# Chunk 0's decays summed in PSUM instead of passed through DRAM, the beginning reordered, and the check of the weights moved to later chunks

## The chip, the core and the metric

The kernel runs on one core of a Trainium2 chip. The metric is the device time of one execution in microseconds (us), median over runs. Names: PE is TensorE, DVE is VectorE, ACT is ScalarE, POOL is GpSimd, SP is SyncE, which here only issues DMAs. Each engine executes its own instructions in the order in which they stand in its queue.

## The reference, cut to what is computed

```python
for t in range(S):                                  # B, H, S, D = 4, 8, 768, 40
    m_new = np.maximum(f_gate[:, :, t] + m, i_gate[:, :, t])
    f_stab = np.exp(f_gate[:, :, t] + m - m_new);  i_stab = np.exp(i_gate[:, :, t] - m_new)
    m = m_new
    C = f_stab * C + i_stab * einsum('bhd,bhe->bhde', vt, kt);  n = f_stab * n + i_stab * kt
    y[:, :, t] = sigmoid(o_gate) * (C @ qt) / np.maximum(np.abs(n . qt), 1.0)
x = y.transpose(0, 2, 1, 3).reshape(B * S, H * D)   # 3072 x 320
h = x @ w_in;  x = (h - np.tanh(h)) @ w_out          # 320 -> 2048 -> 320
...                                                 # then top-1 routing to 8 experts,
out[mask] = gate_w[mask, None] * (np.maximum(x[mask] @ w1[e], 0) @ w2[e])   # 320 -> 1024 -> 320
```

`w_in` and `w_out` come as 64-bit floats (`in_w64`), all else as 32-bit.

## The kernel before, in words

The sequence is cut into 6 chunks of 128 positions. A chunk has 4 units, one for each batch entry, and a unit has two halves (even and odd heads, 4 heads each). Attention of chunk c+1 is woven into the first GEMM pair (320 to 2048 to 320) of chunk c. That pair has 16 steps a chunk, one for each block of 128 of the 2048; in step n PE does the second product of step n (`gemm2`, L191 to L193) and the first product of step n+3 (`gemm1`, L183), while ACT and DVE make the activation of the steps between (`g_chain`, L207 to L210, and `g_split`, L215 and L160). H0 below is the first `gemm1` of all, H16 the first of chunk 1. After each chunk `route` (L675 on) copies the result out, works out each row's expert and scatters the rows to `xs`. After chunk 5 come the experts (from 531.9 us).

Work before H0 is attention of chunk 0. For each half unit:
- the decay matrix D, 128 x 4 x 128. It is exp(g_t + b_s) where t is not before s, else 0. g and b are the gates' running sums (`gates`, L443 on, DVE): g is written to DRAM (`gd`, L468) and loaded back spread over 128 partitions (`load_d`, L401, 256 KB a half); b is turned to a column by PE (L476, ACT L477 `bcol`). ACT takes four exponentials of 128 x 128, with b as bias (L524), and POOL puts 0 above the diagonal (L525 `affine_select`);
- `scores`: products of q and k into PSUM `ps` (L520), behind two idle products (`warm`, L734) a bank;
- `weigh`: A = ps * D (DVE L536), and kw = k * last column of D (POOL L534 in chunk 0);
- `outs`: kw and A against v (PE L550 `po`, L554 `pi`); `sums`: dn from pi (DVE L577 to L579), z = sigmoid(o) * dn (POOL L581), the state C (ACT L586); `finish`: y = pi * z (DVE L596, L598); `turn`: y transposed (PE L604 `px`); `low`: its high and low part (ACT L609 `xh`, DVE L611 `xl`), into `xT`. H0 needs `xl` of all 4 units.

`prep(f)` readies block f of the 64-bit weights: a 704 KB load (`raw`, L441, two buffers), three DVE operations that cut it to 32 bits (L312 to L314), a check on ACT that all values are small (L646 square, L647 exponential with a sum into `wsum`), and at the next call the split into high and low part (ACT L172 and L173, POOL L160 three times). `gemm1(f)` needs it.

The beginning is written out by hand: `LOADS` is the order of its loads and gate steps, `START` that of its compute, both up to the `|` in `START`; `S W O M F U L` are the unit's steps just named (`S00` is unit 0, half 0), `P` calls `prep`, `G` the next part of `gates`, `I0` and `I1` the sigmoids of the o gates of chunk 0 and 1 (`s0`, `s1`, 640 KB each; `u` loads a unit's q, k and v, `w` a raw block, `e` some small constants), `D4 D5` load units 4 and 5, `E` is `setup`, `H C X` are `gemm1`, `g_chain` and `g_split`. Behind the `|` the framework's scheduler sets each engine's order, by its own estimate, from the order of the program, and can move instructions far ahead. `plan` and the `PLACE` tables say at which step attention comes.

Of the kernel before, what the change touches and what calls it, by code (L numbers as in the profile page):

```python
# [40 lines left out]
LOADS = 'g c i u0 G d0 u1 d1 s0 w0 u2 d2 w1 u3 d3 Q s1 e'  # L41
# [67 lines left out]
def build(ctx, tc, qk, vk, og, gat, w64, w12, emb, tau, cst, tok, empty, out):  # L109
# [27 lines left out]
    wsum = const.tile([128, NF], F32, tag="wsum", name="wsum")  # L137
# [306 lines left out]
    def gates():  # L444

        f, i = gts[0], gts[1]
        m = attp.tile([32, S], F32, tag="sg", name="gm", bufs=1)
        g = attp.tile([32, S], F32, tag="T", name="gg", bufs=1)
        for c0, c1 in ((0, 1), (1, NCH)):
# [11 lines left out]
            for c in range(c0, c1):
                sl = slice(c * L, (c + 1) * L)
                V.tensor_tensor_scan(out=g[:, sl], data0=f[:, sl], data1=f[:, sl], initial=0.0, op0=ALU.add, op1=ALU.bypass)
            V.tensor_tensor(out=f[:, a:z], in0=i[:, a:z], in1=m[:, a:z], op=ALU.subtract)
            V.tensor_tensor(out=f[:, a:z], in0=f[:, a:z], in1=g[:, a:z], op=ALU.subtract)
            if c0:
# [172 lines left out]
    def prep(f):  # L639
# [303 lines left out]
    for n in range(NS + NE):  # L943
# [232 lines left out]
```

## Time and profile before

| | us |
|---|---|
| median of 3 runs (766.13 to 771.18) | 767.34 |
| the profiled execution's own time | 767.0 |
| its span, first to last instruction | 765.2 |
| H0 starts | 59.65 |
| H16 starts | 154.70 |
| first copy out of `route`, chunks 0 to 5 | 163.3, 241.7, 319.5, 396.6, 466.5, 531.9 |

All times in rows are from the span's start, of that one execution. PE is busy 93% of the span, DVE 75%, ACT 59%, POOL 24%. A busy share is a mean over stages, so the rows are read stage by stage. Ends of PE's matmuls are modelled, and its busy time includes overlaps of neighbours. The granted TensorE clock is a fraction of 2.4 GHz (0.5 is the lower level, 1.2 GHz).

### The profile page before, as it was taken

How to read it: one execution, taken by the hardware profiler on the slowest of the kernel's cores; microseconds unless marked ns; L12 is line 12 of the kernel's file. 1: busy time of each engine (PE TensorE's matmuls, PEld its weight loads, DVE VectorE, ACT ScalarE, POOL GpSimd, SP SyncE). 2: the span in 40 equal slices, each digit the busy share in tenths (PEclk: the TensorE clock that was granted, in tenths of full speed). 3: DMA queues.
4: the chain of work that ended last, by engine and by line, in shares of the span. 5: the costliest groups of instructions: out<-in, count | busy, mean ns of one | idle time of the engine just before them, and what ended most of it. 6: DMA issues, size and time to landing. Idle time of an engine off the chain costs nothing. (4 is left out here: it accounts for less than half of the span.)

```text
span 765.2 us, 15047 instructions
## 1 busy us (share of the span) xinstructions
PE 708.6 (93%) x5310; PEld 622.4 (81%) x5312; DVE 570.8 (75%) x1464; ACT 448.9 (59%) x1079; POOL 180.5 (24%) x231
## 2 busy tenths in 40 slices
PE   6648899899999999999999998899999999999993
PEld 3436677788888888888888887788999899999993
DVE  5386999979987999699879988987638755556320
ACT  3686597794568555855585447667447545545321
POOL 2293265521132113120201022210221102202111
PEclk9557999999999999999999999999999999999997
DMA  7766778532242224322332012026356735534000
GB/s 238 263 199 231 251 241 278 178 93 82 80 151 85 81 74 124 109 82 82 122 120 73 18 49 72 1 74 198 121 171 214 223 110 161 177 98 157 26 23 23
DMA packets 47286, 98.59 MB, mean 129 GB/s; under 512 B 13278, under 2 KB 21641, under 8 KB 46544
## 3 DMA queue, kind: packets, MB, share of 16 engines
q1 hardware_dynamic: 44496, 89.44, 36.3%
q0 software_dynamic: 2512, 7.89, 2.7%
q8 instruction: 44, 0.72, 0.4%
q14 instruction: 42, 0.34, 0.1%
q10 hardware_dynamic: 192, 0.20, 0.1%
HBM read 85.57 MB, written 17.87 MB: 135 GB/s over the span
## 5 line engine op out<-in xcount | busy, mean ns | idle before, releaser
L183 PE MATMUL h<-xh,wi 128*128 128x512 f32 (+6 forms) x880 | 296.0, 374 | 7.2 <-DVE glo L160 3.8
L191 PE MATMUL acc<-wo,ghi 128*128 128x320 f32 (+1 forms) x616 | 197.3, 321 | 4.8 <-ACT ghi L215 4.3
L183 PEld LDWEIGHTS h<-xh,wi 128*128 128x128 f32 x880 | 165.3, 191 | 34.3 <-DVE glo L160 7.1
L183 PE MATMUL h<-xl,wi 128*128 128x512 f32 (+6 forms) x528 | 192.4, 369 | 0.1
L192 PE MATMUL acc<-wo,ghi 128*128 128x320 f32 (+1 forms) x616 | 190.4, 310 | 0.0
L193 PE MATMUL acc<-wo,glo 128*128 128x320 f32 (+1 forms) x616 | 187.0, 310 | 0.0
L191 PEld LDWEIGHTS acc<-wo,ghi 128*128 128x128 f32 (+1 forms) x616 | 114.3, 186 | 11.2 <-ACT ghi L215 6.6
L192 PEld LDWEIGHTS acc<-wo,ghi 128*128 128x128 f32 (+1 forms) x616 | 114.4, 186 | 2.9 <-issue 0.2
L193 PEld LDWEIGHTS acc<-wo,glo 128*128 128x128 f32 (+1 forms) x616 | 113.8, 186 | 2.5 <-issue 0.3
L215 ACT ACTIVATE ghi<-h 128x512 fp32r<-128x512 f32 x96 | 56.8, 592 | 93.9 <-DVE h L210 65.8
L183 PEld LDWEIGHTS h<-xl,wi 128*128 128x128 f32 x528 | 101.1, 191 | 11.2 <-DVE xl L611 1.1
L877 DVE SCALAR_TENSOR_TENSOR glo<-h,ghi 128x256 fp32r<-128x256 f32 (+5 forms) x80 | 41.3, 516 | 60.4 <-ACT ghi L876 59.2
L209 DVE SCALAR_TENSOR_TENSOR s<-s,u 128x512 f32<-128x512 f32 x96 | 69.0, 718 | 21.2 <-ACT s L208 20.8
L525 POOL TENSOR_SCALAR_AFFINE_SELECT D<-D 128x512 f32<-128x512 f32 x48 | 36.9, 770 | 179.7 <-ACT D L524 109.8
L207 ACT ACTIVATE u<-h 128x512 f32<-128x512 f32 x96 | 57.0, 593 | 36.4 <-PE h L183 34.2
L160 DVE TENSOR_TENSOR glo<-h,ghi 128x512 fp32r<-128x512 f32 x96 | 65.8, 685 | 16.5 <-ACT ghi L215 12.3
L260 DVE SCALAR_TENSOR_TENSOR jk<-R,enb 128x320 bf16<-128x320 f32 x152 | 77.5, 510 | 0.4 <-ACT R L675 0.2
L524 ACT ACTIVATE D<-D,bcol 128x128 f32<-128x128 f32 x192 | 63.1, 391 | 22.8 <-DMA D<-gd 19.0
L876 ACT ACTIVATE ghi<-h 128x256 fp32r<-128x256 f32 (+5 forms) x80 | 36.7, 459 | 66.5 <-PE acc L192 66.3
L208 ACT ACTIVATE s<-u,cs 128x512 f32<-128x512 f32 x96 | 69.0, 719 | 0.9
L160 DVE TENSOR_TENSOR wi<-ew,wi 128x256 fp32r<-128x256 f32 (+1 forms) x128 | 46.2, 361 | 27.8 <-ACT wi L172 26.7
L210 DVE SCALAR_TENSOR_TENSOR h<-s,h 128x512 f32<-128x512 f32 x96 | 66.0, 688 | 0.8
(180 smaller groups left out, 916.4 us busy)
## 6 DMA issues: line engine op xcount, KB each, us to landing
ew<-in_w SPq DMA_DIRECT2D x64, 352.0 KB, 3.0
D<-gd SPq DMA_DIRECT2D x48, 256.0 KB, 3.4
raw<-in_w SPq DMA_DIRECT2D x16, 704.0 KB, 5.7
W<-in_qk SPq DMA_DIRECT2D x20, 512.0 KB, 3.9
vk<-in_vk SPq DMA_DIRECT2D x20, 324.0 KB, 3.7
xs<-blank SPq DMA_DIRECT2D x32, 161.0 KB, 4.2
sg<-in_og SPq DMA_DIRECT2D x6, 640.0 KB, 5.2
ys<-y SPq DMA_DIRECT2D x24, 160.0 KB, 2.4
```

The lines of the kernel that those rows point to most:

```text
L160: eng.tensor_tensor(out=out, in0=x, in1=hi.bitcast(F32), op=ALU.subtract)
L183: MM(h[:, 0:cols], wi[:, k, :], x[:, kk, :], start=n == 0, stop=n == len(seq) - 1)
L191: MM(o, ghi[:, sl], wo[:, 0, 0:320], start=first, stop=False)
L192: MM(o, ghi[:, sl], wo[:, 1, 0:320], start=False, stop=False)
L193: MM(o, glo[:, sl], wo[:, 0, 0:320], start=False, stop=last)
L207: A.activation(out=u, in_=h, func=AF.Square, accum_out=usum[:, n:n + 1])
L208: A.activation(out=s, in_=u, func=AF.Square, bias=col(C_BETA))
L209: V.scalar_tensor_tensor(out=s, in0=s, scalar=GAMMA, in1=u, op0=ALU.add, op1=ALU.mult)
L210: V.scalar_tensor_tensor(out=h, in0=s, scalar=C2, in1=h, op0=ALU.mult, op1=ALU.mult)
L215: A.activation(out=ghi, in_=g, func=AF.Copy)
L260: V.scalar_tensor_tensor(out=jk[1], in0=x2, scalar=1.0, in1=enb[:, e, :], op0=ALU.mult, op1=ALU.mult, accum_out=lg[:, j, e:e + 1])
L524: A.activation(out=Dt[:, j, :], in_=Dt[:, j, :], func=AF.Exp, bias=bcol[:, k:k + 1])
```

## The change

In chunk 0, g no longer goes through DRAM. The gate inputs are loaded twice, on partitions 0 to 31 and 32 to 63. DVE multiplies g by a 0/1 pattern of heads and b by a 0/1 pattern of groups (`rowsel`), and for each half unit PE forms g_t + b_s in a PSUM bank by one product over 64 rows (L416), adding a mask of -1e30 above the diagonal by a second product in bf16 (L417). One exponential (L558) makes D of the half. ACT and POOL make the patterns and the mask once (`masks`). The rotation of PSUM banks in the beginning gets an eighth bank. `LOADS` and `START` are rewritten. The check leaves `prep`: the high words are loaded again, half a block at a time (`load_high`, 32 loads of 352 KB, two buffers under the tag `wf`), and checked (`small`) in steps 16 to 79 of the program. The blank rows of `xs` are written in chunk 1's steps of the program instead of chunk 0's. DVE's, POOL's and ACT's work in later attention is unchanged.

```diff
-LOADS = 'g c i u0 G d0 u1 d1 s0 w0 u2 d2 w1 u3 d3 Q s1 e'
+LOADS = 'g c i Z s0 u0 I0 G G G u1 w0 u2 w1 u3'
-START = ('S00 S01 W00 S10 S11 W01 W10 P W11 G I0 I1 O0 M0 S21 S20 P O1 W20 S30 F0 W21 S31 M1 P U0 W30 O2 F1 U1 W31 O3 L0 M2 P F2 M3 U2 L1 '
-         'L2 D4 F3 D5 U3 G L3 H0 E | H1 s00 w00 s01 C0 H2 X0 w01 C1 o0 m0 f0 u0 P l0')
+START = ('B0 S00 S01 B1 W00 W01 S10 S11 P W10 W11 O0 M0 G G +s1 +e B2 S20 S21 F0 O1 W20 W21 M1 U0 B3 S30 S31 F1 O2 W30 '
+         'W31 L0 M2 U1 O3 F2 L1 U2 M3 P F3 L2 U3 D4 D5 L3 H0 P H1 C0 G P E I1 | H2 X0 C1 s00 s01 w00 w01 o0 m0 f0 u0 P '
+         'l0 ')
...
+    def masks():
+        G.memset(causal, 0.0)
+        G.affine_select(out=causal, in_=causal, pattern=[[1, L]], compare_op=ALU.is_ge, fill=-1.0e30, base=0, channel_multiplier=-1)
+        A.activation(out=hidden, in_=causal.unsqueeze(1).to_broadcast([128, 4, L]), func=AF.Copy)
+        A.activation(out=groups[0:32], in_=cs[0:32, C_GRP:C_GRP + 8].unsqueeze(2).to_broadcast([32, 8, L]), func=AF.Copy)
+        A.activation(out=heads[32:64], in_=cs[32:64, C_HEAD:C_HEAD + 4].unsqueeze(2).to_broadcast([32, 4, L]), func=AF.Copy)
+        A.activation(out=identb, in_=ident, func=AF.Copy)
+    def spread(b):
+        for par in range(2):
+            pb = Db[b, par] = at_bank("pb")
+            MM(pb, groups[:, 2 * b + par, :], heads.rearrange("p j t -> p (j t)"), start=True, stop=False)
+            MM(pb, identb, hidden.rearrange("p j t -> p (j t)"), start=False, stop=True)
...
+            if c0 == 0:
+                V.tensor_tensor(out=heads[0:32], in0=g[0:32, 0:L].unsqueeze(1).to_broadcast([32, 4, L]),
+                                in1=cs[0:32, C_HEAD:C_HEAD + 4].unsqueeze(2).to_broadcast([32, 4, L]), op=ALU.mult)
+                for r in (slice(0, 2), slice(2, 8)):
+                    V.tensor_tensor(out=groups[32:64, r, :], in0=f[32:64, 0:L].unsqueeze(1).to_broadcast([32, r.stop - r.start, L]),
...
+                if c == 0:
+                    Dt = v['D', par] = wpool.tile([128, 4, L], F32, tag="wi", name="D")
+                    A.activation(out=Dt, in_=Db.pop((b, par)).rearrange("p (j t) -> p j t", j=4), func=AF.Exp)
+                    return
...
-        A.activation(out=jw, in_=hi, func=AF.Square)
-        A.activation(out=jw, in_=jw, func=AF.Exp, scale=-131072.0, accum_out=wsum[:, f:f + 1])
...
+    def load_high(f):
+        t = wk.tile([128, WC], U32, tag="wf", name="high", bufs=2)
+        nc.sync.dma_start(out=t, in_=w64[f // 2, :, f % 2 * WC:(f % 2 + 1) * WC])
+        raw_t[f] = t.rearrange("p (c two) -> p c two", two=2)[:, :, 1].bitcast(F32)
+    def small(f):
+        jw = wk.tile([128, WC // 2], BF16, tag="jw", name="jw")
+        A.activation(out=jw, in_=raw_t.pop(f), func=AF.Square)
+        A.activation(out=jw, in_=jw, func=AF.Exp, scale=-131072.0, accum_out=wsum[:, f:f + 1])
...
+        if NF <= n < 5 * NF:
+            k = n // 2 - NF // 2
+            if n % 2 == 0:
+                load_high(k)
+            else:
+                small(k)
...
-        if n < NF:
-            for r in range(2 * f, 2 * f + 2):
+        if NF <= n < NF + 8:
+            for r in range(4 * f, 4 * f + 4):
```

Three places show what this moves. The first is SP's queue in the beginning, behind the two loads of constants. Here it stands before (`ue` are q, k and v of a unit, `D` the spread decays, `sg_198` the o gate of chunk 0):

```order
L416 DMA ue<-in_qk 128x512 x2
L416 DMA ue<-in_vk 128x328
L416 DMA ue<-in_vk 128x320
L468 DMA gd<-gg 32x128
L401 DMA D<-gd 128x512 x2
L416 DMA ue<-in_qk 128x512 x2
L416 DMA ue<-in_vk 128x328
L416 DMA ue<-in_vk 128x320
L401 DMA D<-gd 128x512 x2
L429 DMA sg_198<-in_og 128x1280
L441 DMA raw<-in_w 128x1408
```

And here it stands now (`sg_162` is the o gate of chunk 0):

```order
L455 DMA sg_162<-in_og 128x1280
L442 DMA ue<-in_qk 128x512 x2
L442 DMA ue<-in_vk 128x328
L442 DMA ue<-in_vk 128x320
L442 DMA ue<-in_qk 128x512 x2
L442 DMA ue<-in_vk 128x328
L442 DMA ue<-in_vk 128x320
L467 DMA raw<-in_w 128x1408
```

The o gate moved ahead of the first unit, and the write of g and the eight loads of D are gone, so that units stand behind units and blocks of weights.

The second place is DVE's queue at the end of chunk 0's attention, up to the last `xl`. The rows with `t_787` and `t_835` are blocks 4 and 5 of the weights before:

```order
L313 SCALAR_TENSOR_TENSOR t_787<-raw,t_787 128x704
L578 TENSOR_TENSOR dn<-pi,dn 128x8
L314 SCALAR_TENSOR_TENSOR wf<-raw,t_787 128x704
L579 RECIPROCAL dn<-dn 128x8
L611 TENSOR_TENSOR xl<-px,xh 128x3x128 x2
L312 TENSOR_SCALAR t_835<-raw 128x704
L596 TENSOR_TENSOR y<-pi,z 128x320
L313 SCALAR_TENSOR_TENSOR t_835<-raw,t_835 128x704
L598 COPY y<-y 128x64
L314 SCALAR_TENSOR_TENSOR wf<-raw,t_835 128x704
L486 COPY eGL<-pl 104x80
L611 TENSOR_TENSOR xl<-px,xh 128x3x128
```

Now `t_546` is block 1 and `t_598` block 2, and the last row is the first of `g_chain` behind H0:

```order
L618 RECIPROCAL dn<-dn 128x8
L318 TENSOR_SCALAR t_546<-raw 128x704
L319 SCALAR_TENSOR_TENSOR t_546<-raw,t_546 128x704
L320 SCALAR_TENSOR_TENSOR wf<-raw,t_546 128x704
L635 TENSOR_TENSOR y<-pi,z 128x320
L637 COPY y<-y 128x64
L650 TENSOR_TENSOR xl<-px,xh 128x3x128 x2
L318 TENSOR_SCALAR t_598<-raw 128x704
L319 SCALAR_TENSOR_TENSOR t_598<-raw,t_598 128x704
L320 SCALAR_TENSOR_TENSOR wf<-raw,t_598 128x704
L215 SCALAR_TENSOR_TENSOR s<-s,u 128x512
```

Two blocks of weights stand ahead of the last `xl` now, where six stood before; four moved behind H0.

The third place is ACT's queue in chunk 1, some steps of the GEMM pair (`ghi`, `u` and `s` are its activation, numbered). Before:

```order
L207 ACTIVATE u_2025,usum_88<-h_2002 128x512
L215 ACTIVATE ghi_2016<-h_1949 128x512
L208 ACTIVATE s_2026<-u_2025,cs_81 128x512
L524 ACTIVATE D_2092<-D_2092,bcol_109 128x128 x4
L207 ACTIVATE u_2102,usum_88<-h_2043 128x512
L215 ACTIVATE ghi_2052<-h_2002 128x512
L208 ACTIVATE s_2103<-u_2102,cs_81 128x512
L215 ACTIVATE ghi_2143<-h_2043 128x512
L207 ACTIVATE u_2155,usum_88<-h_2134 128x512
L208 ACTIVATE s_2156<-u_2155,cs_81 128x512
```

And now, at about the same steps (`jw` are the checks):

```order
L699 ACTIVATE jw_2821,wsum_88<-jw_2821 128x352
L698 ACTIVATE jw_2943<-high_2878 128x352
L699 ACTIVATE jw_2943,wsum_88<-jw_2943 128x352
L221 ACTIVATE ghi_2083<-h_1972 128x512
L213 ACTIVATE u_2095,usum_88<-h_2070 128x512
L698 ACTIVATE jw_3085<-high_2992 128x352
L214 ACTIVATE s_2096<-u_2095,cs_80 128x512
L699 ACTIVATE jw_3085,wsum_88<-jw_3085 128x352
L698 ACTIVATE jw_3190<-high_3127 128x352
L699 ACTIVATE jw_3190,wsum_88<-jw_3190 128x352
L698 ACTIVATE jw_3330<-high_3237 128x352
L221 ACTIVATE ghi_2154<-h_2070 128x512
```

The scheduler moved the checks far ahead of their places in the program: in ACT's whole queue 3 stand ahead of chunk 0's copy out, 25 between that and chunk 1's (18 of them within 8 steps), and 4 behind it.

## Rows read from the trace of the kernel before

**Rows 1.** Busy time of each engine (instructions), granted clock, DMA, by stage.
```profile
core 0: us, PE busy (x) PEld busy (x) DVE busy (x) ACT busy (x) POOL busy (x), PEclk, DMA share, GB/s
0.00:59.65 59.65, 35.13 (x319) 23.05 (x321) 36.60 (x71) 35.39 (x84) 29.24 (x43) 0.66 0.69 239
59.65:154.70 95.05, 85.77 (x644) 69.85 (x644) 83.30 (x148) 68.88 (x168) 43.20 (x54) 0.92 0.69 231
87.90:143.40 55.50, 50.71 (x362) 41.57 (x359) 52.36 (x84) 44.38 (x104) 28.53 (x32) 0.97 0.78 263
163.30:241.70 78.40, 76.28 (x655) 65.65 (x654) 68.55 (x200) 48.75 (x120) 17.87 (x22) 1.00 0.32 101
```

**Rows 2.** Waits from 0 to 59.65: who for whom, us, times, longest.
```profile
ACT sg L435 <- DMA sg<-in_og: 5.9, 1, 5.9
DVE A L536 <- POOL D L525: 12.6, 3, 9.1
```

**Rows 3.** Timeline: start, us, engine, line, operation [idle before, releaser].
```profile
31.44 1.27 ACT L435 ACTIVATE sg<-sg 128x1280 f32<-128x1280 f32 x1 [5.88 <-DMA sg<-in_og]
33.24 1.28 ACT L524 ACT_TABLE_LOAD   x1
37.72 0.69 DVE L536 TENSOR_TENSOR A<-ps,D 128x512 f32<-128x512 f32 x1 [9.12 <-POOL D L525]
12.96 1.14 DVE L465 TENSOR_TENSOR gat<-gat,gg 32x640 f32<-32x640 f32 x1
7.14 1.54 DVE L451 TENSOR_TENSOR_SCAN gm<-gat,gm 32x640 f32<-32x640 f32 x1 [1.32 <-DMA gat<-in_gat]
```

**Rows 4.** Groups by line from 0 to 59.65: busy, mean ns | idle before.
```profile
L524 ACT ACTIVATE D<-D,bcol 128x128 f32<-128x128 f32 x32 | 9.9, 387 | 5.7 <-DMA D<-gd 5.7
L554 PE MATMUL pi<-ue,A 128*64 128x41 f32 x128 | 8.0, 308 | 0.0
L314 DVE SCALAR_TENSOR_TENSOR wf<-raw,t 128x704 uint32<-128x704 uint32 x6 | 6.2, 1040 | 0.9 <-POOL wo L160 0.7
L525 POOL TENSOR_SCALAR_AFFINE_SELECT D<-D 128x512 f32<-128x512 f32 x8 | 6.2, 771 | 24.9 <-ACT D L524 24.9
L313 DVE SCALAR_TENSOR_TENSOR t<-raw,t 128x704 uint32<-128x704 uint32 x6 | 6.1, 1024 | 0.1
L520 PE MATMUL ps<-ue 40*128 40x128 f32 x64 | 6.5, 361 | 3.3 <-DMA ue<-in_qk 3.3
L536 DVE TENSOR_TENSOR A<-ps,D 128x512 f32<-128x512 f32 x8 | 5.5, 685 | 12.6 <-POOL D L525 12.6
L734 PE MATMUL ps<-busy,oneb 128*128 128x512 bf16 x14 | 5.4, 482 | 3.8 <-ACT C L586 3.6 <-issue 0.2
L550 PE MATMUL po<-ue,kw 128*40 128x41 f32 x64 | 4.2, 274 | 7.1 <-POOL kw L534 7.1
L604 PE MATMUL px<-cs,y 128*128 128x128 f32 x12 | 4.0, 438 | 8.9 <-DVE y L596 8.0 <-DVE y L598 0.7
L312 DVE TENSOR_SCALAR t<-raw 128x704 uint32<-128x704 uint32 x6 | 3.9, 643 | 2.9 <-DMA raw<-in_w 2.9
```

**Rows 5.** The check's two operations over the whole span: ns min/median/max, first and last start.
```profile
L646 ACT ACTIVATE jw<-raw x16: 825/837/873, 20.7 to 139.2; 128x704 bf16<-128x704 f32 x16
L647 ACT ACTIVATE jw<-jw x16: 773/787/791, 21.6 to 140.2; 128x704 bf16<-128x704 bf16 x16
L647 ACT ACTIVATION_READ_ACCUMULATOR jw<-jw x16: 185/188/200, 22.3 to 140.9; 128x1 f32 x16
```

**Rows 6.** DMA issues: line, count, KB each, median us to landing.
```profile
ew<-in_w SPq DMA_DIRECT2D x64, 352.0 KB, 3.0
sg<-in_og SPq DMA_DIRECT2D x6, 640.0 KB, 5.2
```

**Rows 7.** One operation of `prep` over the whole span, as in rows 5.
```profile
L313 DVE SCALAR_TENSOR_TENSOR t<-raw,t x16: 873/892/1566, 21.3 to 140.3; 128x704 uint32<-128x704 uint32 x16
```

**Rows 8.** The page's group of the square of a 128 x 512 PSUM bank.
```profile
L207 ACT ACTIVATE u<-h 128x512 f32<-128x512 f32 x96 | 57.0, 593 | 36.4 <-PE h L183 34.2
```

More of the change, by code (lines that the diff above doesn't have):

```diff
@@ L79 @@
 C_BETA2 = C_CAP + 8
-C_ID = C_BETA2 + 1
+C_HEAD = C_BETA2 + 1
+C_GRP = C_HEAD + 4
+C_ID = C_GRP + 8
 C_SEL = C_ID + 128
@@ L124, in build @@
     blank = dram.tile([128, XW], F32, tag="blank", name="blank")
-    gd = [dram.tile([NCH - 1 if k else 1, B * H * L], F32, tag=f"gd{k}", name="gd") for k in range(2)]
+    gd = dram.tile([NCH - 1, B * H * L], F32, tag="gd", name="gd")
     ys = dram.tile([NT, DM], F32, tag="ys", name="ys")
@@ L136, in build @@
     usum = const.tile([128, NCH * NF], F32, tag="usum", name="usum")
[L137 removed]
+    wsum = const.tile([128, 2 * NF], F32, tag="wsum", name="wsum")
     def col(i, n=1, p0=0, p1=128):
@@ L384, in load_gates @@
         for k in range(2):
-            gts[k] = attp.tile([32, S], F32, tag="W", name="gat")
+            gts[k] = attp.tile([64, S], F32, tag="W", name="gat")
             A.dma_start(out=gts[k][:, 0:L], in_=gat[:, k, 0:L])
         for k in range(2):
-            A.dma_start(out=gts[k][:, L:S], in_=gat[:, k, L:S])
+            A.dma_start(out=gts[k][0:32, L:S], in_=gat[0:32, k, L:S])
+    rowsel = xp.tile([64, 12, L], F32, tag="xl", name="rowsel")
+    groups, heads = rowsel[:, 0:8, :], rowsel[:, 8:12, :]
+    hidden = chain.tile([128, 4, L], BF16, tag="s", name="hidden", bufs=1)
+    identb = chain.tile([128, L], BF16, tag="ghi", name="identb")
+    causal = chain.tile([128, L], F32, tag="glo", name="causal")
+    Db = {}
+    def masks():
[10 more added lines that the diff above has]
+            MM(pb, identb, hidden.rearrange("p j t -> p (j t)"), start=False, stop=True)
     def load_d(i):
@@ L444, in gates @@
     def gates():
[L446 to L449, printed above, removed]
+        m = attp.tile([64, S], F32, tag="sg", name="gm", bufs=1)
+        g = attp.tile([64, S], F32, tag="T", name="gg", bufs=1)
+        for c0, c1, rw in ((0, 1, 64), (1, NCH, 32)):
             a, z = c0 * L, c1 * L
-            V.tensor_tensor_scan(out=m[:, a:z], data0=f[:, a:z], data1=i[:, a:z],
-                                 initial=-1.0e30 if c0 == 0 else m[:, a - 1:a], op0=ALU.add, op1=ALU.max)
+            f, i = gts[0][0:rw], gts[1][0:rw]
+            V.tensor_tensor_scan(out=m[0:rw, a:z], data0=f[:, a:z], data1=i[:, a:z],
+                                 initial=-1.0e30 if c0 == 0 else m[0:rw, a - 1:a], op0=ALU.add, op1=ALU.max)
             if c0 == 0:
@@ L462, in gates @@
                 sl = slice(c * L, (c + 1) * L)
[L463 to L466, printed above, removed]
+                V.tensor_tensor_scan(out=g[0:rw, sl], data0=f[:, sl], data1=f[:, sl], initial=0.0, op0=ALU.add, op1=ALU.bypass)
@@ L467, in gates @@
                 yield
-            nc.sync.dma_start(out=gd[c0][:, :].rearrange("c (r t) -> r c t", r=32), in_=g[:, a:z].rearrange("r (c t) -> r c t", t=L))
-            if c0:
-                yield
+                continue
+            yield
+            nc.sync.dma_start(out=gd[:, :].rearrange("c (r t) -> r c t", r=32), in_=g[0:32, a:z].rearrange("r (c t) -> r c t", t=L))
+            yield
             n = 32 * (c1 - c0)
             pt = at_bank("pt")
-            for x, o in ((f, 0), (g, n))[0:c1]:
+            for x, o in ((f, 0), (g, n)):
@@ L701, in load @@
         elif op == 'G':
-            run(gt, 3)
-        elif op == 'Q':
             run(gt)
+        elif op == 'Z':
+            masks()
+        elif op == 'I':
+            sigm(s_t[k])
         elif op == 'd':
@@ L787, in build @@
             gt = run(gt)
+        elif op == 'B':
+            spread(int(k))
+        elif op == 'Z':
+            masks()
+        elif op == '+':
+            load(k)
         elif op == 'D':
```

36 lines of the change are left out of this document (20 added, 16 removed).

## The prediction

> **What bounds the kernel now.** I read busy time by stage first [rows 1]. From chunk 1 on PE is busy 76.28 of 78.40 us at the full granted clock: there it is the bound, at 78.4 / 16 = 4.9 us a step, and another engine matters only where it makes PE wait. Up to H0 no engine is near full: PE 35.13, DVE 36.60, ACT 35.39 of 59.65 us. That stage is a chain of waits. From H0 to H16, which by chunk 1's pace would be 16 x 4.9 = 78 us, it is 95.05 us, and in the part from 87.90 to 143.40 DVE is busy 52.36 of 55.50, or 94.3%: nine blocks of weights are cut there, one in 6.2 us, and DVE is the bound.
>
> The second view is the waits up to H0 [rows 2]. DVE waits 12.6 us for D, 9.1 of it at once; ACT waits 5.9 us for the o gate of chunk 1. The timeline [rows 3] shows that they are one story: at 31.44 ACT gets that o gate at last, takes its sigmoid, loads the other table, and then makes the exponentials of unit 2, so that DVE's product for unit 2 starts only at 37.72. The group of the exponentials [rows 4] has 5.7 us more of waiting for D's own DMA.
>
> **The change, part by part.** I make the sum against the profiled execution's own 767.0 us; the median is 767.34, so 0.3 more. A measurement of this kernel can tell about 1%, 7.7 us, from no change.
>
> *Up to H0.* Removed are 32 exponentials of 387 ns (9.9 us) and eight of POOL's 771 ns [rows 4], the wait for chunk 1's sigmoid [rows 2], eight loads of 256 KB, and six checks of 837 + 787 + 188 = 1.81 us [rows 5]. Added are eight exponentials of 128 x 512; their price lies between 0.59 us, the square of such a bank [rows 8], and four old ones, 1.55 us [rows 4]. I take 0.59, the row of the same size and source.
>
> Now the new chain. DVE's gates ended at 14.10 us 12.96 + 1.14 [rows 3]. New in front of them are products of 512 + 256 + 768 elements, 2.05 us by 685 ns for 512 [rows 4], of which 1.32 us fills a wait for the gates' load [rows 3]. So the gates end at 14.8, and the two A of unit 0 at 16.2. What must be there by then: chunk 0's o gate is the first large load and lands within about 5.2 us of issue [rows 6], say 7 us; two table loads of 1.28 and a sigmoid of 1.27 [rows 3] and two exponentials make 12. ACT's copies for the masks lie beside the gates. This cover is 2.8 us; if the o gate is later than that, H0 is later by the rest.
>
> From 16.2 to H0 stands the work of PE, since DVE has less: 36.60 [rows 1] less four blocks of weights that moved behind H0 (0.643 + 1.024 + 1.040 = 2.71 us each [rows 4], 10.8) plus 2.05, so 27.8 us in all, done by about 33 if nothing held it. PE has `pi` 8.0, `po` 4.2, `px` 4.0, half of `ps` 3.3, eight idle products of 0.482 = 3.9 [rows 4], and the products for D of units 2 and 3. No row has these. A product in plain 32 bits leaves two records (64 of L520 for 32 products [rows 4]); if a record costs as much as a bank's 482 ns [rows 4], one half is 3 x 0.482 = 1.45 us with its mask, and four are 5.8. The sum is 29.2 us, H0 at 45.4, at a clock whose mean was 0.66 [rows 1]. If all ran at the full level it would be 29.2 x 0.66 = 19.3, H0 at 35.5; if DVE's block of weights (2.71) and a z come on top in the last unit, 49. PE will be denser than before and so should be granted more; against that, the four units still hand over between PE, DVE and POOL. I take 43, nearer the late end. Gain: 59.65 - 43 = 16.7 us (bounds 10.7 to 24).
>
> A rule bears on the products for D. By the Trainium skill, FP8 and Floating Point Precision, section TensorE Precision Notes, true FP32 takes four passes through the array. The two records do not say how many passes each holds. By that rule each half costs two passes, 0.96 us, more; that is a rival below.
>
> *From H0 to H16.* DVE had 83.30 us of work [rows 1] and gets four blocks, 10.8 us, more: 94.1. ACT loses some ten checks (18 us) and gains four splits and chunk 1's sigmoid. If DVE is as full as where it was the bound, 94.3% [rows 1], the stage is 99.8 us; at 100% 94.1; at the old 87.6% (83.30 / 95.05) 107.4. I take 99.8, as ACT, the engine that DVE waited for, has less to do. That gives back 99.8 - 95.05 = 4.7 us of the 16.7. Net: H16 at 142.8 in place of 154.7, 12.0 us earlier.
>
> *The check in later steps.* Each of 32 costs a square and an exponential of 352 elements, half of 704: 0.42 + 0.39 + 0.19 = 1.00 us by halves, at most the old 1.81 [rows 5]; I take 1.1, since an operation's cost does not fall all the way with its size. The order shows 25 of them between the copies out of chunk 0 and 1, where ACT is busy 48.75 of 78.40 [rows 1]: 48.75 + 27.5 = 76.3, just below the stage. But 18 of them stand in 8 steps: per step 48.75 / 16 = 3.05 us and 2.25 x 1.1 = 2.5 more make 5.5, against PE's 4.9. Eight steps of 0.6 are 4.9 us; PE has about a step of slack, as H is started three steps ahead, so I take 2.0 (bounds 0 to 12, the far end with waits for loads as in the third rival). Their 11.3 MB lie beside a DMA share of 0.32 [rows 1].
>
> *At nothing*: the doubled gate rows (partitions run side by side), the eighth bank, later blank rows of `xs`, the wider `wsum`; the covers are DVE's gates and SP's idle queue. Without the cover each is under 1 us.
>
> Sum: 767.0 - 16.7 + 4.7 + 2.0 = 757.0.
>
> **Rivals.**
>
> *Both early stages go better.* PE is granted the full level most of the way to H0 (H0 at 39.5), and DVE is 98% full behind it (96.0 us): H16 at 135.5, 19.2 us earlier. With 0.2 for the checks: 748. For it: six checks and four splits leave ACT and POOL before H0. Against it: clock 0.66 in a stage with as many hand-overs.
>
> *DVE gives most of it back.* DVE stays at 87.6% behind H0: 107.4, so H16 at 150.4, 4.3 earlier, and with 2.0 for the checks 765. For it: the same operation on the same 704 elements took from 873 to 1566 ns [rows 7], and four more blocks are split by POOL beside DVE now. By the Trainium skill, GPSIMD Engine Reference, section 1. Specifications, POOL shares its SBUF interfaces with DVE where DVE reads two SBUF inputs, as here; the rows agree as far as the spread goes, and the rule speaks against moving POOL's splits beside DVE's busiest time.
>
> *Four passes.* 0.96 us more for each half: 3.8 us for units 2 and 3, and units 0 and 1 no longer fit in front of 16.2 (about 1 us). H0 at 48: 762.
>
> *Slower: ACT stands waiting for the high words.* There are two buffers, and in SP's queue their loads stand behind loads that wait for PE and DVE. Where 2.25 checks come in a step of 4.9 us, one comes each 2.2 us, while one load takes 3.0 us to land at the same 352 KB [rows 6] and its buffer is free only after a square of 0.42. If the two buffers do not overlap, since the second load is held up in the queue, a check waits 3.0 + 0.42 - 2.2 = 1.2 us with the GEMM's activation behind it, 18 x 1.2 = 22 us, and PE pays it once its step of slack is gone: 757 - 2 + 22 = 777. It decides from about 1.1 us a check. Against it: loads of a like size run far ahead in chunk 1 at a DMA share of 0.32 [rows 1].
>
> **How the numbers follow.** Forecast 757, own range 751 to 762: 0.47. Better: 0.20. Gives back: 0.18. Four passes: 0.09. Slower: 0.06. The range 745 to 768 takes in all but the slower rival and the edges of the others. Faster by over 1% is below 759.7: most of the forecast (0.41), the better case (0.20) and a part of four passes (0.03) and of the third (0.01), 0.65; slower 0.06; within 1% the rest, 0.29.
>
> **What would show it.** Right: ACT's wait for the o gate and DVE's wait for POOL's D are gone from the waits; the first `gemm1` starts at 40 to 46; DVE is over 92% busy from there to H16, which starts near 143; chunk 1 lasts 79 to 82 us, with PE waiting for ACT's `ghi` or DVE's `glo` a little. Wrong: a wait of ACT for the high words above 8 us in chunk 1, or of DVE for ACT's D before H0; a stage from H0 to H16 shorter than 94 us, which DVE's 94.1 us of work forbids unless its operations get shorter; or a product for D whose records are above 0.9 us.

## The result and the profile after

The changed kernel takes 759.75 us (median of 4, 757.2 to 760.43) where the kernel before took 767.68 beside it: ratio 0.9884 (95% interval 0.9843 to 0.9926), 1.2% faster. Beside other runs of before it was 0.9890 (0.9864 to 0.9917). The forecast was 757.0. The experiments ran in other sets of runs, in which before itself took 778 and 771 us, so that each is read by its ratio to before in the same runs, or by stages of its own profile. Two of them had times far above their others, which the comparisons leave out (without idle products two of four, 11 to 17 us above; with the gate early again one of ten, 9 us above its median), and as the profile of the first is of such a run, no row of it is used.

The profiled execution took 760.43 us. Busy time by stage of the changed kernel, which answers to [rows 1]: up to H0, from H0 to H16, from H0 to the first copy out of chunk 0 (the boundary used for the experiments), and chunks 1 and 2 from first copy to first copy.

```profile
core 0: us, PE busy (x) PEld busy (x) DVE busy (x) ACT busy (x) POOL busy (x), PEclk, DMA share, GB/s
0.00:41.98 41.98, 33.73 (x335) 18.06 (x339) 28.22 (x61) 18.15 (x34) 12.66 (x24) 0.94 0.58 193
41.98:143.09 101.11, 88.64 (x650) 71.50 (x651) 92.85 (x161) 63.95 (x157) 54.53 (x66) 0.92 0.80 270
41.98:152.95 110.97, 98.34 (x756) 79.80 (x756) 99.42 (x176) 73.11 (x175) 55.63 (x68) 0.93 0.78 262
152.95:235.43 82.48, 76.13 (x648) 64.00 (x647) 68.87 (x193) 70.84 (x194) 14.73 (x21) 1.00 0.63 192
235.43:314.36 78.93, 75.46 (x655) 64.86 (x654) 68.87 (x197) 51.93 (x132) 15.54 (x21) 1.00 0.37 112
```

H0 came 17.7 us earlier; the stage behind it gave back 6.1, and H16 came 11.6 earlier. ACT's work in chunk 1 rose from 48.75 [rows 1] to 70.84. The whole difference of the two profiled executions, in which the later rows are differences of first copies (before: 163.31, 241.72, 319.47, 531.90):

| part | forecast, us | measured, us |
|---|---|---|
| up to H0 | -16.7 | 41.98 - 59.65 = -17.67 |
| H0 to H16 | +4.7 | 101.11 - 95.05 = +6.06 |
| H16 to the first copy | 0 | 9.86 - 8.61 = +1.25 |
| chunks 1 and 2 | +2.0 | (82.48 - 78.41) + (78.93 - 77.75) = +5.25 |
| chunks 3 to 5 | 0 | 213.19 - 212.43 = +0.76 |
| experts | 0 | 232.88 - 235.10 = -2.22 |
| sum | -10.0 | 760.43 - 767.00 = -6.57 |

The waits up to H0, which answer to [rows 2] (who for whom, us, times, longest): neither ACT's wait for an o gate nor DVE's for POOL's `D` is among them. The longest that are left of DVE and of PE:

```profile
DVE A L575 <- PE ps L555: 4.6, 2, 3.0
PE px L643 <- DVE y L635: 4.0, 1, 4.0
```

The timeline, as in [rows 3]: the sigmoid of chunk 0's gate, the last operation of a block of weights, then unit 3's `y`, and the transposes that wait for it.

```profile
8.29 1.27 ACT L461 ACTIVATE sg<-sg 128x1280 f32<-128x1280 f32 x1
38.26 1.29 DVE L320 SCALAR_TENSOR_TENSOR wf<-raw,t 128x704 uint32<-128x704 uint32 x1
39.48 0.48 DVE L635 TENSOR_TENSOR y<-pi,z 128x320 f32<-128x320 f32 x1
40.02 0.69 PE L643 MATMUL px<-cs,y 128*128 128x128 f32 x2 [4.04 <-DVE y L635]
```

The block stands in DVE's queue in front of `y`, and PE waits 4.04 us: that is the last hold-up before H0. What the new operations cost, by the groups up to H0 (beside [rows 4]) and by PE's timeline of unit 0:

```profile
L416 PE MATMUL pb<-rowsel 64*128 64x512 f32 x16 | 8.8, 633 | 1.2 <-DVE rowsel L498 0.7 <-issue 0.5
L558 ACT ACTIVATE D<-pb 128x512 f32<-128x512 f32 x8 | 4.8, 597 | 8.1 <-PE pb L417 5.2 <-remote 2.2 <-PE pt L511 0.8
...
8.94 1.09 PE L416 MATMUL pb<-rowsel 64*128 64x512 f32 x2 [0.67 <-DVE rowsel L498]
9.97 0.39 PE L417 MATMUL pb<-hidden,identb 128*128 128x512 bf16 x1
10.29 1.12 PE L416 MATMUL pb<-rowsel 64*128 64x512 f32 x2
11.57 1.03 PE L783 MATMUL ps<-busy,oneb 128*128 128x512 bf16 x4
12.53 0.72 PE L555 MATMUL ps<-ue 40*128 40x128 f32 x8
```

From its start to the mask's a product takes 9.97 - 8.94 = 1.03 us; with the mask a half takes 10.29 - 8.94 = 1.35 (forecast 1.45), and the exponential 0.597 (forecast 0.59).

The check now, by line over the whole span (ns min/median/max, first and last start; beside [rows 5]), its loads (KB each, median us to landing), and of chunk 1 ACT's wait for its loads, SP's wait for ACT's checks, and the two longest of PE:

```profile
L698 ACT ACTIVATE jw<-high x32: 504/522/563, 134.7 to 252.1; 128x352 bf16<-128x352 f32 x32
L699 ACT ACTIVATE jw<-jw x32: 479/497/535, 136.5 to 252.7; 128x352 bf16<-128x352 bf16 x32
L699 ACT ACTIVATION_READ_ACCUMULATOR jw<-jw x32: 185/188/239, 136.9 to 253.1; 128x1 f32 x32
high<-in_w SPq DMA_DIRECT2D x32, 352.0 KB, 3.7
...
ACT jw L698 <- DMA high<-in_w: 7.0, 5, 2.7
SPq L692 <- ACT jw L698: 25.4, 22, 4.8
PE px L643 <- DVE A L575: 2.5, 2, 1.7
PE h L189 <- DVE glo L166: 2.1, 2, 1.9
```

A check is 0.52 + 0.50 + 0.19 = 1.21 us. PE is idle for 82.48 - 76.13 = 6.35 us of chunk 1, where it was for 2.1 before [rows 1].

### The profile page after: what moved, and what is told of

It is laid out like the page before. It is cut to its first block, busy times and chain, and to the rows that moved or that the text cites. A ratio compares the mean times of both kernels' runs of the same rounds, so it can differ in the third digit from the quotient of the medians.

```text
span 758.7 us, 15147 instructions
## 1 busy us (share of the span) xinstructions
PE 707.6 (93%) x5332; PEld 616.0 (81%) x5335; DVE 574.2 (76%) x1467; ACT 453.3 (60%) x1108; POOL 169.2 (22%) x225
## 5 line engine op out<-in xcount | busy, mean ns | idle before, releaser
L564 POOL TENSOR_SCALAR_AFFINE_SELECT D<-D 128x512 f32<-128x512 f32 x40 | 28.8, 721 | 159.2 <-ACT D L563 77.7
L563 ACT ACTIVATE D<-D,bcol 128x128 f32<-128x128 f32 x160 | 53.2, 392 | 17.5 <-DMA D<-gd 10.6
```

What stands on the lines that cost most here:

```text
L563: A.activation(out=Dt[:, j, :], in_=Dt[:, j, :], func=AF.Exp, bias=bcol[:, k:k + 1])
```

## The experiments

Theories at the start. Q: the loss in chunk 1 is the checks standing in ACT's queue. M: it is their loads. N: it is something else. For the stage behind H0: DVE's work sets it (the forecast's view), or PE's clock does.

**No check.** The step's calls of `load_high` and `small` are dropped and `wsum` is set to 0. It ran twice.

```diff
-        if NF <= n < 5 * NF:
-            k = n // 2 - NF // 2
-            if n % 2 == 0:
-                load_high(k)
-            else:
-                small(k)
...
+    G.memset(wsum, 0.0)
```

> Leaves out the check of the weights and its 32 loads (the sums it writes are set to 0). Of the changed kernel chunk 1 (first copy out of chunk 0 to first copy out of chunk 1) took 82.5 us where it took 78.4 before, and chunk 2 78.9 where 77.75. Theory Q: the checks stand in ACT's queue in front of the GEMM's activation; without them chunk 1 is 78.4 to 79.0 us, chunk 2 77.8, and the run 5 us shorter than the changed kernel, about 755. Rival N, the loss comes from something else that the change moved into chunk 1 (the blank rows of xs, chunk 1's units): chunk 1 stays at 82 or more and the run at 760.

> The changed kernel without the checks once more, since the profiled run of the first time was 9 us above its own median. The two medians of that chip, 767.4 here and 769.8 with the checks, make the checks 2.4 us; the comparison of chunk 1 before and after makes them 4 to 5. By the first theory the ratio to before is again about 0.987; by the second 0.983 or less, with PE idle in chunk 1 for 2 us as before the change where the changed kernel has 6.4.

First 767.4 us, ratio 0.9866 (0.9811 to 0.9922), with a profiled run 9 us above its median; then 760.0, ratio 0.9861 (0.9836 to 0.9886). Chunk 1 of the first, of the second, and of a kernel with the checks in the second's set of runs (the one with the gate early again, below):

```profile
154.59:238.18 83.59, 79.62 (x660) 68.06 (x660) 70.35 (x202) 47.56 (x120) 17.50 (x22) 0.98 0.33 100
...
153.72:232.48 78.76, 77.26 (x660) 66.61 (x660) 69.98 (x202) 47.65 (x120) 17.17 (x22) 1.00 0.33 105
...
154.44:237.81 83.37, 80.71 (x662) 69.15 (x661) 70.88 (x204) 72.68 (x194) 16.96 (x22) 0.98 0.66 203
```

In the second profile chunk 1 is 3.7 us shorter than with the checks (82.48), and 4.6 shorter than with them in the same set of runs (at a clock of 1.00 for 0.98), and PE's idle time in it is 1.5 us; chunk 2 was 79.14, as with them (78.93). So this profile speaks against N for chunk 1 and for a cost of the checks of about 4 us. The first profile does not show it: in a run that was long as a whole, chunk 1 took 83.59 us without any check, and chunk 2 83.38. What they cost of the total is less certain: 0.9884 - 0.9861 and 0.9890 - 0.9866 are both some 0.24%, 1.8 us, and the intervals overlap, so that no cost in the total is shown beyond doubt. My estimate from these is 2 to 4 us.

**Loads without checks**, to tell Q from M: the call of `small` alone is dropped, and `wsum` set to 0.

> The 32 loads of high words stay, the check's two operations on ACT are left out (its sums are set to 0). Theory Q: chunk 1 is 78.4 to 79.2 us, as without any of it, total about 755. Rival M, the extra 11.3 MB beside the loads of units and of D: chunk 1 stays at 81 to 82.5, total 758 to 760, with waits of ACT for D's DMA or of PE for W's above 1.5 us.

776.42 us, ratio 0.9973 (0.9943 to 1.0003): worse than the changed kernel, though ACT does nothing of the check.

```profile
153.15:243.98 90.83, 80.96 (x660) 69.07 (x660) 70.09 (x202) 47.51 (x119) 18.39 (x22) 0.96 0.61 186
...
SPq L692 <- DMA high<-in_w: 31.5, 20, 5.3
ACT D L563 <- DMA D<-gd: 12.8, 3, 4.7
PE h L189 <- DVE glo L166: 6.0, 2, 3.0
```

Chunk 1 is longer than either branch of the expectation had it. With no reader to hold them, loads follow one another in SP's queue as fast as they land (20 waits of SP for the load before, 31.5 us in all), and the loads of `D` behind them come late: ACT waits 12.8 us for them, 1.7 in the changed kernel. Loads alone can cost more than the whole check, so M is a real mechanism. In the changed kernel ACT's checks hold the loads back (SP waits 25.4 us for them), and ACT itself waits 7.0 us for the words.

**Thin checks**: each reads 8 columns of 352, so that ACT waits for every load but works less.

```diff
-        A.activation(out=jw, in_=raw_t.pop(f), func=AF.Square)
-        A.activation(out=jw, in_=jw, func=AF.Exp, scale=-131072.0, accum_out=wsum[:, f:f + 1])
+        A.activation(out=jw[:, 0:8], in_=raw_t.pop(f)[:, 0:8], func=AF.Square)
+        A.activation(out=jw[:, 0:8], in_=jw[:, 0:8], func=AF.Exp, scale=-131072.0, accum_out=wsum[:, f:f + 1])
```

> Each check reads 8 of its 352 columns, so that ACT still waits for each load in its order but works some 0.5 us less on each (32 x 0.5 = 16 us in all; ACT busy in chunk 1 about 60 in place of 70.8). If theory Q is a matter of ACT's waits for the words (7.0 us in chunk 1), chunk 1 stays at 81 to 82.5; if it is a matter of ACT's work, it falls to 78.5 to 79.5 and the run to 755 to 756.

772.36 us, ratio 0.992 (0.9889 to 0.995). Chunk 1, in a profiled run 4.6 us above the median:

```profile
156.11:242.86 86.75, 80.06 (x660) 68.11 (x660) 70.41 (x202) 60.69 (x207) 17.71 (x22) 0.98 0.66 208
```

ACT's work in it fell to 60.69 us as expected, its waits for the words rose to 9.6, chunk 1 was longer than either branch had it, and the run is not shorter than the changed kernel's 0.9890. So less of ACT's work alone shows no gain. That does not say how much of chunk 1's loss the waits are, since the loads can start at other times when ACT frees their buffers sooner.

**One check in every second step.** `last[0]` is the `ghi` of the step.

```diff
+    last = [None]
...
-        A.activation(out=ghi, in_=g, func=AF.Copy)
+        last[0] = A.activation(out=ghi, in_=g, func=AF.Copy)
...
-                small(k)
+                with tc.issue_after(last[0].ins):
+                    small(k)
```

> Each check is tied behind the ghi of its own step, so that one stands in every second step from chunk 1 to 4 where 18 stood in 8 steps. Theory Q: chunk 1 is 78.4 to 79.3, chunks 2 to 4 at most 0.4 longer each than before the change (77.75, 77.1, 69.85), total 755 to 756. If what counts is the check's sum and not its crowding, chunks 1 to 4 lose 5 us together all the same and the run stays at 759 to 760. Rival M: chunk 1 near 79.5, with the rest of the loss in later chunks.

769.45 us, ratio 0.9896 (0.984 to 0.9951): no gain is shown. Its chunk 1:

```profile
150.76:233.90 83.14, 79.55 (x667) 68.01 (x666) 72.35 (x205) 55.71 (x145) 18.00 (x24) 1.00 0.44 130
```

No ACT wait for the words is left in chunk 1 and PE's idle time there falls to 83.14 - 79.55 = 3.6 us, but from the beginning of step 16's activation to the first copy of chunk 5 it takes 389.0 us, and the changed kernel, in another set of runs in which before took 778 us too, 389.1. That looks like the second branch of the expectation, the sum of the checks spread over four chunks, but it does not show it: the first profile without any check takes 390.6 us for the same stretch.

**The changed kernel again**, beside the next three.

> The changed kernel once more, beside the three below, since the first experiments ran where before itself took 778 us. Theory: the stages keep their order: H0 at 42, first copy out of chunk 0 about 153, chunk 1 longer than before's 78.4 by 4 us, 1.0 to 1.3% faster than before. If chunk 1 is here no longer than chunk 2, the loss in chunk 1 was chance.

769.82 us, ratio 0.9890. H0 was at 41.23, the first copy at 155.37, chunk 1 83.69 and chunk 2 81.39 us. So the order of the stages repeats, while single stages differ from the first profile by up to 3.2 us.

**The second block of weights earlier.** `N` makes DVE's part of a block without the splits of earlier ones, `Q` the splits alone.

```diff
-START = ('B0 S00 S01 B1 W00 W01 S10 S11 P W10 W11 O0 M0 G G +s1 +e B2 S20 S21 F0 O1 W20 W21 M1 U0 B3 S30 S31 F1 O2 W30 '
-         'W31 L0 M2 U1 O3 F2 L1 U2 M3 P F3 L2 U3 D4 D5 L3 H0 P H1 C0 G P E I1 | H2 X0 C1 s00 s01 w00 w01 o0 m0 f0 u0 P '
+START = ('B0 S00 S01 B1 W00 W01 S10 S11 P W10 W11 O0 M0 G G +s1 +e B2 S20 S21 F0 O1 W20 W21 M1 U0 B3 S30 S31 F1 N O2 W30 '
+         'W31 L0 M2 U1 O3 F2 L1 U2 M3 Q F3 L2 U3 D4 D5 L3 H0 P H1 C0 G P E I1 | H2 X0 C1 s00 s01 w00 w01 o0 m0 f0 u0 P '
...
```

> The second block of weights before H0 is made at once behind unit 1's y, where DVE waited 3.0 us for PE, and no longer in front of unit 3's y (PE waited 4.0 us for that y, 36.43 to 39.48 were the block). Theory: H0 falls by 2.1 us, from 42.0 to 39.9; as DVE is what fills the stage behind, with the same work in it, H16 falls by as much, 143.1 to 141. Rival: PE or ACT sets that stage, and H16 stays at 143.

766.28 us, ratio 0.9863 (0.9822 to 0.9903). H0 and the stage to the first copy, of this kernel and then of the changed kernel beside it:

```profile
0.00:40.02 40.02, 33.84 (x338) 18.05 (x339) 27.09 (x61) 18.77 (x35) 11.37 (x24) 0.96 0.71 237
40.02:151.75 111.73, 100.46 (x756) 82.61 (x756) 97.57 (x176) 72.21 (x174) 57.08 (x69) 0.89 0.74 248
...
41.23:155.37 114.14, 101.38 (x756) 82.22 (x756) 100.50 (x176) 73.07 (x176) 53.89 (x68) 0.90 0.74 255
```

On DVE's timeline unit 2's `y` now waits until an earlier `y` is written out:

```profile
35.40 0.49 DVE L635 TENSOR_TENSOR y<-pi,z 128x320 f32<-128x320 f32 x1 [2.44 <-DMA ys<-y]
```

So H0 fell by 1.2 us, not 2.1; the first copy came 3.6 earlier, and the run is 3.5 shorter by the medians, while the intervals of the ratios overlap. What is gained up to the first copy reaches the end here. The stage itself is 2.4 us shorter, and its 176 operations of DVE took 2.9 us less. That this comes from the edit is not shown: six profiles of kernels that differ in this stage by the checks alone have 110.97 to 114.35 us.

**Fewer idle products.**

```diff
-                        warm(v['ps', p])
+                        warm(v['ps', p], None if b == 0 or c else 0)
```

> The idle products are left out for units 1 to 3 of chunk 0 (12 of 512 columns, 4 in 1.03 us of PE's queue). From 12.5 to 34.8 PE has no idle time to speak of, so by the theory that PE is the bound there H0 falls by 3.1 us, to 38.9, and H16 by as much, with the clock at 0.94 in that stage as before. Rival, the idle products hold the clock up: mean clock to H0 below 0.9 and H0 at 42 or later.

Four times, 766.29, 770.75, 782.02 and 783.35; ratio 0.9878 (0.9841 to 0.9915) of those that count. Inconclusive: neither a gain nor a loss against the changed kernel is shown.

**Three edits together**: checks tied to their steps, the block earlier, fewer idle products.

> The three edits together: each check tied behind its own step's ghi, the second block of weights behind unit 1's y, no idle products for units 1 to 3. Theory: chunk 1 and 2 lose 4 us less, H0 is at 37 and H16 at 138: 4 + 5 = 9 us less than the changed kernel in the same runs. Rival, the stage behind H0 gives it all back: 4 us less.

763.72 us, ratio 0.9836 (0.9806 to 0.9867), against 769.82 for the changed kernel and 777.85 for before in the same runs: the fastest of all, 6 us better than the change. H0 is at 38.83 and the first copy at 148.07, 7.3 us before the changed kernel's; from there on nothing more is gained. The gain expected of the checks (4 us) did not come, that of the beginning did, though H0 was to be at 37. Unit 3's last `pi` ends at 31.57, where the kernel with the block alone earlier has 33.82: leaving out 3.1 us of idle products brought PE on by 2.2. Of that 1.2 us reach H0, as unit 2's `y` now waits 3.31 us, in place of 2.44, until an earlier `y` is written out:

```profile
34.20 0.49 DVE L637 TENSOR_TENSOR y<-pi,z 128x320 f32<-128x320 f32 x1 [3.31 <-DMA ys<-y]
```

**Before with the o gate alone moved**, the kernel before with chunk 1's gate loaded and its sigmoid taken behind H0.

```diff
-LOADS = 'g c i u0 G d0 u1 d1 s0 w0 u2 d2 w1 u3 d3 Q s1 e'
+LOADS = 'g c i u0 G d0 u1 d1 s0 w0 u2 d2 w1 u3 d3 Q e'
-START = ('S00 S01 W00 S10 S11 W01 W10 P W11 G I0 I1 O0 M0 S21 S20 P O1 W20 S30 F0 W21 S31 M1 P U0 W30 O2 F1 U1 W31 O3 L0 M2 P F2 M3 U2 L1 '
-         'L2 D4 F3 D5 U3 G L3 H0 E | H1 s00 w00 s01 C0 H2 X0 w01 C1 o0 m0 f0 u0 P l0')
+START = ('S00 S01 W00 S10 S11 W01 W10 P W11 G I0 O0 M0 S21 S20 P O1 W20 S30 F0 W21 S31 M1 P U0 W30 O2 F1 U1 W31 O3 L0 M2 P F2 M3 U2 L1 '
+         'L2 D4 F3 D5 U3 G L3 H0 E I1 | H1 s00 w00 s01 C0 H2 X0 w01 C1 o0 m0 f0 u0 P l0')
```

> The kernel before with one part of the change alone: chunk 1's o gate is loaded and its sigmoid taken only behind H0. Theory: the wait of 5.9 us at 31.4, a sigmoid and two table loads (3.8 us) leave ACT's queue in front of unit 2's exponentials, so that H0 comes 6 to 9 us earlier, at 51 to 54, a third to a half of the changed kernel's 17.7; the rest is D's. Rival: the loads of D by DRAM are next in line (5.7 us of waits of ACT for them) and H0 stays at 57 or later.

765.29 us, ratio 0.9921 (0.9892 to 0.9951). The stage up to H0, the stage behind it to the first copy (and the same stage of the kernel before), and the waits up to H0:

```profile
0.00:52.42 52.42, 32.89 (x322) 21.50 (x322) 36.24 (x71) 34.24 (x83) 29.52 (x43) 0.69 0.77 259
52.42:160.50 108.08, 96.80 (x751) 82.17 (x750) 87.41 (x163) 81.39 (x188) 42.97 (x57) 0.90 0.65 221
...
59.65:163.31 103.66, 94.38 (x741) 77.28 (x741) 87.97 (x157) 77.45 (x183) 43.83 (x55) 0.93 0.66 218
...
PE px L604 <- DVE y L596: 8.3, 2, 5.3
DVE A L536 <- POOL D L525: 6.2, 4, 3.2
ACT D L524 <- DMA D<-gd: 5.4, 3, 2.6
```

H0 comes 7.2 us earlier, and the run is 6 us faster, most of what the whole change brings. The wait for `D` falls from 12.6 us [rows 2] to 6.2. By the first copy 4.4 of the 7.2 us are lost again in this profile (108.08 for 103.66 us, at a clock of 0.90 for 0.93), though no block of weights moved here; the two profiles are of different sets of runs, and where the 6 us of the medians stand is open.

**The changed kernel with that gate early again.**

```diff
-LOADS = 'g c i Z s0 u0 I0 G G G u1 w0 u2 w1 u3'
+LOADS = 'g c i Z s0 u0 I0 G G G u1 w0 u2 w1 u3 s1'
-START = ('B0 S00 S01 B1 W00 W01 S10 S11 P W10 W11 O0 M0 G G +s1 +e B2 S20 S21 F0 O1 W20 W21 M1 U0 B3 S30 S31 F1 O2 W30 '
-         'W31 L0 M2 U1 O3 F2 L1 U2 M3 P F3 L2 U3 D4 D5 L3 H0 P H1 C0 G P E I1 | H2 X0 C1 s00 s01 w00 w01 o0 m0 f0 u0 P '
+START = ('B0 S00 S01 B1 W00 W01 S10 S11 P W10 W11 O0 M0 G G +e I1 B2 S20 S21 F0 O1 W20 W21 M1 U0 B3 S30 S31 F1 O2 W30 '
+         'W31 L0 M2 U1 O3 F2 L1 U2 M3 P F3 L2 U3 D4 D5 L3 H0 P H1 C0 G P E | H2 X0 C1 s00 s01 w00 w01 o0 m0 f0 u0 P '
```

> The changed kernel with chunk 1's o gate early again, its load behind unit 3's and its sigmoid ahead of unit 2's products for D. Theory: the load lands by 24, ACT loses 3.8 us and a wait of 1 to 2, and unit 2's two A, which have some 5 us before PE asks for them, hide most of it: H0 at 42 to 44.5. Rival: the deferral was the larger part of the gain with D in PSUM too: H0 at 48 or later, and ACT's wait for that load above 5 us.

H0 at 41.44, as without it, and ACT's wait for the gate is 1.0 us, in front of the table load for its sigmoid:

```profile
21.34 1.28 ACT L461 ACT_TABLE_LOAD   x1 [0.99 <-DMA sg<-in_og]
```

So in the changed kernel the order of this load no longer matters to H0. The run is 766.54 us, ratio 0.9943 (0.9921 to 0.9966), 0.5% worse than the changed kernel all the same. The profiled run was the shortest of ten, and shows no place for that; it stays open.

**POOL makes chunk 1's `kw`.**

```diff
-KW_POOL = (0, 2, 3, 4, 5)
+KW_POOL = (0, 1, 2, 3, 4, 5)
```

> POOL makes chunk 1's eight kw in place of DVE (8 x 0.50 = 4.0 us of DVE's work between H0 and H16). If DVE's work sets that stage, it is 3 to 4 us shorter, about 97 where the two profiles of the changed kernel have 101 and 103, and the run 2 to 4 us faster than it (1.4 to 1.6% faster than before). Rival: POOL beside DVE stretches DVE's other operations by as much as it takes off, or PE's clock sets the stage, and it stays at 101 to 103.

764.72 us, ratio 0.9924 (0.99 to 0.9949): not faster than the changed kernel. The profiled run, at 770.26 us, is the longest of five. Its stage from H0 to the first copy, and three windows in it:

```profile
41.58:159.04 117.46, 102.74 (x745) 84.66 (x746) 96.82 (x164) 71.31 (x172) 59.81 (x74) 0.87 0.74 246
...
120.00:125.00 5.00, 3.75 (x21) 2.74 (x20) 5.00 (x10) 2.83 (x7) 3.10 (x3) 1.00 0.86 225
125.00:130.00 5.00, 2.51 (x41) 2.06 (x39) 5.00 (x8) 2.60 (x9) 2.51 (x3) 0.98 0.89 299
130.00:135.00 5.00, 5.00 (x42) 4.49 (x43) 4.44 (x7) 2.47 (x6) 3.73 (x4) 0.50 0.37 90
```

DVE's work fell to 96.82 us from 99.42 and 100.50 in the two profiles of the changed kernel, and the stage grew from 110.97 and 114.14 to 117.46, at a clock of 0.87 (0.93 and 0.90 there). In the windows DVE is full for 10 us, PE idle for a part of them, and then PE works for 5 us without a gap at half clock. So less of DVE's work did not make the run faster. That it made the stage longer is not shown: the three profiles of the stage grow longer as their clock falls, and what this edit does at an equal clock no run tells.

## Why the prediction was right, point by point

*Up to H0* (forecast -16.7, measured -17.7). The chain held as it was told: both waits are gone, the prices of the new operations were right, unit 0's two `A` ended at 18.0 where I had 16.2, as DVE's gates took longer. From 12.5 to 34.8 us PE had hardly a gap (21.57 of 22.27 us busy) and set the pace; the three edits together bear this out in part, as there 3.1 us less of PE's work ended it 2.2 us earlier. The clock was 0.94 where 0.66 had been; the bound that assumed the full level was 35.5. What made up the difference was the later start and the last unit, where a block of weights came on top, as the late bound had it; that bound's `z` did not, as it ran beside the block and ended at 37.49. So 43 lay near because it stood between two bounds of which each held in a part of the stage, and in that the closeness is luck.

The moved gate and the decays by products overlap. In the kernel before the gate alone gives 7.2 of the 17.7 us, and in the changed kernel it gives H0 nothing. How the other 10.5 us divide is not shown: besides the new way of `D`, four blocks of weights and six checks left this stage, and no run keeps these in place.

*Four passes* was a rival by the wrong price. A product is 1.03 us against 0.24 for an idle product of as many columns in bf16 (four from 11.57 to 12.53): about four times. So the rule of the Trainium skill, FP8 and Floating Point Precision, section TensorE Precision Notes, that FP32 takes four passes, agrees with this trace; two records at 0.482, a row of the stage at low clock, had come to nearly the same sum by chance.

*From H0 to H16* (forecast +4.7, measured +6.1). DVE's work was 92.85 us (forecast 94.1) and its share 91.8% (94.3%, and "over 92%" among the signs). The size was near, and two misses partly cancel: less work of DVE takes 1.3 us off the 99.8, and its lower share adds 2.7. The step in doubt is "If DVE is as full as where it was the bound": that DVE's work sets this stage is argued and not shown, as with less of it the run was not faster. PE's clock is a second term that my sum does not have: with the stage to the first copy at 110.97, 114.14 and 117.46 us, the clock was 0.93, 0.90 and 0.87. It does not account for what the stage gave back, as from H0 to H16 it was 0.92 before [rows 1] and after.

POOL beside DVE does stretch DVE's operations. In the changed kernel's timeline the same operation on a block, without and with POOL beside it:

```profile
19.38 0.89 DVE L320 SCALAR_TENSOR_TENSOR wf<-raw,t 128x704 uint32<-128x704 uint32 x1
...
43.93 1.40 POOL L166 TENSOR_TENSOR wo<-wf,wo 128x320 fp32r<-128x320 f32 x1
44.70 1.37 DVE L320 SCALAR_TENSOR_TENSOR wf<-raw,t 128x704 uint32<-128x704 uint32 x1
```

Of L319's 16 the five with none of POOL's two-input tensor operations (`TENSOR_TENSOR`) beside them take 0.89 us, the seven with such a one beside them for over 0.6 of their time 1.20. Not each is stretched: one of L320's took 0.88 with such an operation beside it nearly throughout. By the Trainium skill, GPSIMD Engine Reference, section 1. Specifications, POOL's SBUF interfaces are shared with DVE, with contention where DVE has two SBUF inputs; the means of this trace agree. It did not bring the rival "DVE gives most of it back" about (87.6%, 765), as DVE was still 91.8% busy, but a part of that busy time is stretch.

*The checks* (forecast +2.0; in the second profile without them chunk 1 is 3.7 us shorter, the total about 2). This is the mis-sized term: "PE has about a step of slack, as H is started three steps ahead, so I take 2.0". A check took 1.21 us where I had 1.1. I priced ACT's work in crowded steps and left the loads to the slower rival (which the sum calls the third; it is the fourth). The runs show that the loads count too: they delay `D` when nothing holds them, and ACT stands 7.0 us for the words when its checks hold them, just short of the 8 us that I had named as a sign against me; chunk 1, at 82.48 us, ended above the 79 to 82 of the signs. The slower rival's mechanism was at work, at 7.0 us of waits where I had priced 22. How chunk 1's loss divides between waits and work is open: with the gate early again the waits were 3.6 us and chunk 1 no shorter (83.37). Of the 5.3 us that chunks 1 and 2 lost, the rest (chunk 2's 1.2 and the remainder of chunk 1's) is not tied to the checks by any run, nor are the 2.2 us that the experts gained. No term of the sum has those 2.2 us, and they cancel a part of what the other stages lost: that the total lay as near as it did is in that part luck.

## What to carry to other kernels

Work that is moved out of a crowded stage to "free" steps brings its loads along: look at where they stand in the queue, and at which loads the bound needs are behind them. When a chain of waits is broken by several edits, try the cheapest edit alone first: here one load, moved with its sigmoid, gave 6 us where the whole change gave about 8. And in a stage where one engine holds PE up, read the granted clock of the next few microseconds too, as the hold-up may be paid again there.

## What was not expected of the hardware

PE's clock after a wait, by windows of 5 us around H0 of the changed kernel:

```profile
30.00:35.00 5.00, 4.77 (x118) 3.92 (x115) 2.38 (x7) 2.75 (x9) 1.18 (x2) 1.00 0.01 2
35.00:40.00 5.00, 0.52 (x3) 0.31 (x3) 4.79 (x11) 0.90 (x3) 3.19 (x4) 0.70 0.00 0
40.00:45.00 5.00, 4.19 (x10) 2.72 (x11) 4.24 (x6) 1.26 (x3) 3.25 (x4) 0.50 0.83 291
45.00:50.00 5.00, 5.00 (x37) 3.81 (x37) 3.57 (x6) 3.97 (x9) 2.27 (x4) 0.78 1.01 330
```

At full level through unit 3, PE waits 4 us for the block in front of `y`, and the first products of the GEMM pair then run at 0.50, the lower of the two levels (1.2 of 2.4 GHz), and 0.78. From 40 to 50 us that is 5 x 0.50 + 5 x 0.22 = 3.6 us of full level not granted (an estimate from these rows), nearly as much again as the wait itself, while PE was busy 4.19 and 5.00 us of the two windows.

The changed kernel took 760 us in one set of runs and 770 in another, and before 767.7 and 778: between sets of runs there is more than the change is worth, and only ratios within a set could be compared.
